# Attention into a top-1 expert layer, fp32, one core: the third batch's turn moved behind the values' products, and three smaller edits

## The chip, the cores and the metric

One core of one Trainium2 chip. The metric is the device time of one execution in microseconds (us); before the change it is 499.81 us, the median of three runs (499.52 to 500.13). Lower is better. Engine names: PE is TensorE's matmul side and PEld its weight loads, DVE is VectorE, ACT is ScalarE, POOL is GpSimd, and SP is the queue of SyncE that issues most transfers.

## The reference

Four batches of 12 heads, 448 positions, 64 values per head: softmax attention whose scores pass through a tanh cap. Its output, 1792 tokens of 768 values, goes through a top-1 layer of eight experts.

```python
scores = (q @ k.transpose(0, 1, 3, 2)) / 8
scores = cap * np.tanh(scores / cap)
attn = softmax(scores)                      # exp over its sum + 1e-9
x = (attn @ v).transpose(0, 2, 1, 3).reshape(1792, 768)
logits = x @ w_gate                         # 8 experts
e = argmax(logits)
out = softmax(logits)[e] * sigmoid(x @ w_output_gate)[e] * (relu(x @ w1[e]) @ w2[e])
```

Each token is computed by its one expert alone, and the expert's weights (w1 768x1024, w2 1024x768 in fp32) are read for the experts that have tokens.

## The kernel before

**Units.** The attention runs over 24 units u, six per batch; a unit is a pair of heads. `qk(u, s)` makes the transposed scores of one slice of keys (slices 0, 1 and 2 hold 128 keys of each head, slice 3 the last 64 of both) and ScalarE's tanh writes them to `pt` (L441). `expo(u)` is one exponential over the whole unit (L444). `pv(u, c)` multiplies by the values (L452), one unit behind the scores: in the loop, unit u's scores come first, then `pv(u - 1)`. `presum(u)` adds up the exponentials (GpSimd up to unit 19, VectorE from 20), and `sums(u)` is a product with a one-hot that collects these sums (L484). `u_evac` moves the values' product from PSUM to `ut`.

**The order is written by hand.** Each engine runs its instructions in the order in which this file emits them. Each unit has places "f", "g", "h", "q" and "e" (`slot(u, y)`): "f" and "g" stand after the scores and before the exponential, "h" after the exponential and before `pv(u - 1)`, "q" after `pv(u - 1)`, "e" at the end of the unit. `end_of_batch(b)` says, in the table `at`, which step of a batch's end goes to which place; a key (x, y) is unit 6(b + 1) + 1 + x, so that (0, ...) is unit 19 and (1, ...) unit 20 for the third batch (b = 2).

**A batch's end** turns the softmax sums into reciprocals, finds each token's expert and writes the token rows:
- `sums_out`: ScalarE copies the sums to `ssb` (L517); `sums_tr`: four PE transposes into `trec` (L522); `recips`: a VectorE reciprocal (L527)
- `gate_mm`, `gate_out`: gate products of three units (`tg`, L536) and ScalarE's copy `gsb` (L295); `gate_tr`, `gate_mul`: PE transposes `pg` (L551), each times the reciprocals on VectorE (L557)
- `logits`, `choose`: VectorE finds the expert (one-hot `ohb`)
- `rank_mm`: two small products with `tri` and `onesb` (`trk`, L597, L598), which also calls `exps` (two small ScalarE exponentials); `place`, `place2`, `enter`: VectorE turns them into table places (`posi`) and entries (`ent`, L629); `scatter`: four indirect GpSimd writes to the tables (L637)
- `row_tr(p)`, `row_out(p)`: for each of six head pairs four PE transposes into `trow` (L646), a VectorE product with the reciprocals into `xr` (L651), and a store of `xr` to `xs` in DRAM, issued on SP when `store_rows` is called (L658). `xr` has three buffers. In the first two batches every other pair is turned on VectorE instead (`row_v`, L682, L684, store L690), with reciprocals from `recips_b` (L677)

**PSUM banks.** In the third batch these PE results take two banks in turn, B and C (`extra`): B is also the bank of slice 1 of the next unit's scores, C that of slice 3. A transposition or a score product into such a bank waits until VectorE or ScalarE has read what stood in it.

**The start.** `load_nat(0)` loads the first keys and queries on the SP and ACT queues; PE turns them (`nat_k`, L414; `nat_q`, L420), and `first_planes(0)` splits them into a high and a low part (K0H, K0L, QH, QL; L295 or L297 and L303). The 64 last keys of the unit are its tails.

**The expert layer.** 13 blocks of 128 tokens (`mm1`, `mm2`, L1175) run on PE; weights come through SP into `raw1`, `raw2` and are split by ScalarE (L1153) and VectorE (L1154) into `wr`. Six smaller rests run beside them (`mm_h`, L1315). Three of the six (`OWN`) have weights of their own, `rh`, six pieces of w1 and eight of w2, loaded on GpSimd's queue (L1291) by `pump`, which is called after each chunk of products and issues one piece at a time when its buffer is used up. `gather_h(k)` fetches a rest's tokens on the same queue (L991 to L1006).

Of the kernel before, what the change touches and what calls it, by code (L numbers as in the profile page):

```python
# [9 lines left out]
F32 = mybir.dt.float32  # L10
# [12 lines left out]
def tile_kernel(ctx: ExitStack, tc, q, k, v, cap, w_gate, w_ogate, w1, w2, out):  # L23
    nc = tc.nc
    B, H, S, D = q.shape
# [74 lines left out]
    NK = 3  # L100
# [10 lines left out]
    def load_natural(dst, src, n, m, engs, lo=0):  # L111
        for j in range(2):
            o = lo if j == 0 else 0
            engs[j].dma_start(out=dst[:, 0:n, j], in_=src[j, o:o + n * m].rearrange("(c p) d -> p c d", c=n))

    def load_nat(u, engs):
        (k0, q0), k_, q_ = nat[u], heads(k, u), heads(q, u)
        load_natural(k0, k_, NK, 128, engs, T0)
        r0, n = u * S, NP * S + SK
        engs[1].dma_start(out=k0[0:64, NK], in_=k.rearrange("b h s d -> (b h s) d")[r0:r0 + 2 * n]  # L120
                          .rearrange("(j r) d -> r j d", j=2)[0:T0])
        load_natural(q0, q_, NCH, CP, engs)

    KT, QT = (0, 1, 4), (2, 3, 5)
    kview = [raw1[i].rearrange("p (h r a) -> p h r a", h=2, a=32) for i in KT]
# [167 lines left out]
    def copy(act, dst, src):  # L293
        if act:
            nc.scalar.activation(out=dst, in_=src, func=ACTF.Copy)  # L295
        else:
            nc.vector.tensor_copy(out=dst, in_=src)  # L297
# [4 lines left out]
    def minus(out, x, y):  # L302
        nc.vector.tensor_tensor(out=out, in0=x, in1=y.bitcast(F32), op=ALU.subtract)  # L303
# [33 lines left out]
    def first_planes(u, mid=lambda: None):  # L337
        ts, (main, *tails) = k_parts(u, nat_k(u))
        if u:
            copy(False, main[0], main[2])  # L340
            minus(main[1], main[2], main[0])
        mid()
        q_, (q0,) = q_parts(u, nat_q(u))
        if u:
            copy(False, q0[0], q0[2])
        else:
            copy(True, main[0], main[2])
            copy(True, q0[0], q0[2])
            minus(main[1], main[2], main[0])
            scales()  # L350
        minus(q0[1], q0[2], q0[0])
        for x, z, y in tails:
            copy(False, x, y)
            minus(z, y, x)
        pl[u] = ts + q_

    def t_k(u):
        pl[u] = planes_of(k_parts(u, turned(ldk.pop(u), SK + 128)))
# [50 lines left out]

    def nat_k(u):  # L410
        pk = tbank([128, S], "tk0")
        for c in range(NK + 1):
            n = min(128, S - c * 128)
            nc.tensor.transpose(pk[:, c * 128:c * 128 + n], nat[u][0][0:n, c].rearrange("p j d -> p (j d)"), ident[0:n, 0:n])  # L414
        return pk
# [87 lines left out]
    def end_of_batch(b):  # L503
# [166 lines left out]
        def recips_b():  # L670
            ps = tbank([128, S], "tks")
            nc.vector.transpose(out=ps, in_=rt["ssb"])
            r = T("recb", [128, NP // 2, NB])
            t = ps.rearrange("p (t r) -> p r t", r=32)
            for a in range(4):
                g = 2 + a // 2
                nc.vector.reciprocal(out=r[32 * a:32 * a + 32], in_=t[32 * g:32 * g + 32, 0:NP // 2])  # L677

        def row_v(p):
            nrow[0] += 1  # L680
# [21 lines left out]
        if b < B - 2:  # L702
            at = {(-2, "q"): [g0], (0, "q"): [g1], (0, "e"): [sums_out], (1, "g"): [t[1], rws[0]], (1, "e"): [recips_b],
                  (2, "e"): [rws[1]], (3, "g"): gts, (3, "e"): [rws[3]], (4, "g"): [rws[2]], (4, "h"): [logits, choose],
                  (5, "g"): [rank_mm, place, place2, rws[4]], (5, "h"): [enter], (6, "e"): [rws[5]]}
            for i, x in enumerate(((6, "g"), (8, "g"), (9, "g"), (10, "g")) if b == 0 else ((6, "g"),) * NCH):
                at.setdefault(x, []).append(P(scatter, (i,)))
        elif b == B - 2:
            g = early()
            nx = P(next, g, None)  # L710
            lds = [P(load_raw, 0, w, c) for w in range(2) for c in range((KD, KF)[w])]
            fd = [P(fetch_dma, i) for i in range(NE)]
            at = {(-2, "q"): [g0], (0, "f"): [P(sums, EARLY), g1, sums_out], (0, "h"): [t[1], *gts, logits, choose],
                  (1, "g"): [rws[0], rank_mm, place], (1, "h"): [place2, enter, scatter], (1, "q"): [rws[1], rws[2], rws[3], store_rows],
                  (2, "g"): [rws[4], rws[5]], (2, "h"): [store_rows, P(v_main, NU - 2, nc.sync), P(v_tails, NU - 2, nc.sync), *[nx] * 6, P(set_known, NE)],
                  (2, "q"): [fd[0], P(v_main, NU - 1, nc.sync), *lds[:2], fd[1]],
                  (3, "h"): [P(gather, 0), P(gather, 1), *lds[2:KD]],
                  (3, "e"): [fd[2], *lds[KD:KD + 2], fd[3]], (4, "f"): lds[KD + 2:]}
# [340 lines left out]
    for u in range(NU):  # L1059
# [7 lines left out]
        if u > 0:  # L1067
            load_ahead()
        if u == 0:
            first_planes(1, lambda: qk(0, NK))  # L1070
        else:
            qk(u, NK if u < NN else 2)
# [220 lines left out]

    def pump():

        if rsp and len(hraw) < len(hseq):
            w = hseq[len(hraw)][0]
            if sum(x[0] == w for x in hraw) - hused[w] < (KD, KF)[w]:
                load_h(len(hraw) + 1)
# [151 lines left out]
```

## Time and profile before

| | |
|---|---|
| median of three runs | 499.81 us |
| the profiled execution | 501.27 us, of which 499.7 us from the first to the last instruction |
| mean granted TensorE clock in it | 0.996 |
| busy, share of the span | PE 97%, DVE 76%, ACT 74%, POOL 59% |

The attention takes the first 189 us of the span, the expert layer the rest. A line of a timeline reads: start in us, duration in us, engine, line of the kernel, operation, tile written <- tiles read, shapes, how many instructions are merged (x4), and in brackets how long the engine sat idle before it and what released it. A product of fp32 tiles counts twice (two passes), so that three products are x6.

### The profile page before, as it was taken

To read this page: it belongs to the slowest core of one execution; us is meant where nothing else is said; L and a number is where in the kernel's file an instruction comes from. 1 tells how busy PE (TensorE), PEld (TensorE's weight loads), DVE (VectorE), ACT (ScalarE), POOL (GpSimd) and SP (SyncE) were. 2 spreads that over 40 slices of the span, in tenths; PEclk is the share of its full clock that TensorE was granted. 3 is DMA by queue.
4 is the path that set the end of the run, shared out by engine and by line. 5 is a ranking of instruction groups with operands and counts; after the bars stand their busy time and mean duration, and the time that the engine had idled before them with its cause. 6 is when DMAs were issued, how large, how long until landed. Compare 5 with 4: busy or idle time off the path is not lost. (4 is left out here: it accounts for less than half of the span.)

```text
span 499.7 us, 9942 instructions
## 1 busy us (share of the span) xinstructions
PE 484.3 (97%) x3040; PEld 335.9 (67%) x3040; DVE 380.4 (76%) x688; ACT 370.0 (74%) x433; POOL 296.0 (59%) x310
## 2 busy tenths in 40 slices
PE   7999999999989999999999999999999899999994
PEld 6544445445445535789998888978799667686691
DVE  6788899999978888999988969758595656565440
ACT  5999999899897797375798878857586666584551
POOL 7899999898998345573758643138356053522001
PEclk9999999999999999999999999999999999999998
DMA  7776777677573669870795263194889599791001
GB/s 175 117 140 114 125 126 136 113 133 115 106 127 55 118 184 335 275 254 1 253 391 220 95 221 134 57 361 168 281 268 407 202 355 411 272 383 46 0 34 53
DMA packets 158590, 91.95 MB, mean 184 GB/s; under 512 B 141234, under 2 KB 141370, under 8 KB 158528
## 3 DMA queue, kind: packets, MB, share of 16 engines
q1 hardware_dynamic: 148544, 58.24, 44.6%
q0 software_dynamic: 8832, 32.74, 17.7%
q8 instruction: 26, 0.43, 0.4%
q10 hardware_dynamic: 1152, 0.25, 0.2%
q14 instruction: 36, 0.29, 0.2%
HBM read 123.68 MB, written 12.04 MB: 272 GB/s over the span
## 5 line engine op out<-in xcount | busy, mean ns | idle before, releaser
L1154 DVE TENSOR_TENSOR wr<-raw,wr 128x768 fp32r<-128x768 f32 (+1 forms) x167 | 171.6, 1066 | 66.4 <-ACT wr L1153 65.6
L1153 ACT ACTIVATE wr<-raw 128x768 fp32r<-128x768 f32 (+1 forms) x167 | 150.3, 935 | 27.4 <-PE py L1175 11.0
L441 ACT ACTIVATE pt<-s,icap 128x896 f32<-128x896 f32 (+1 forms) x95 | 79.4, 917 | 9.2 <-PE s L434 8.2
L452 PE MATMUL u<-pt,vv 128*64 128x448 f32 x384 | 78.2, 546 | 0.5 <-ACT pt L444 0.3
L1175 PE MATMUL py<-wr,hh 128*128 128x384 f32 x352 | 77.3, 340 | 0.0
L1175 PE MATMUL php<-wr,xh 128*128 128x512 f32 x264 | 74.8, 405 | 0.0
L1244 POOL DMA_INDIRECT out_dram<-yo,ti x13 | 20.9, 1610 | 86.3 <-ACT yo L1242 72.3
L444 ACT ACTIVATE pt<-pt,capc 128x3136 f32<-128x3136 f32 x24 | 69.9, 2913 | 0.6
L1175 PEld LDWEIGHTS py<-wr,hh 128*128 128x128 f32 x352 | 61.2, 188 | 4.0 <-issue 3.7
L1175 PEld LDWEIGHTS php<-wr,xh 128*128 128x128 f32 x264 | 47.4, 188 | 12.8 <-issue 2.8
L452 PEld LDWEIGHTS u<-pt,vv 128*64 128x64 f32 x384 | 25.6, 136 | 40.5 <-issue 35.9
L465 POOL TENSOR_TENSOR pb<-pb,pt 64x448 f32<-64x448 f32 x40 | 45.7, 1143 | 3.1
L460 POOL TENSOR_TENSOR pb<-pt 128x896 f32<-128x896 f32 x20 | 42.3, 2113 | 7.8 <-ACT pt L444 4.1
L1175 PE MATMUL py<-wr,hl 128*128 128x384 f32 x176 | 44.8, 335 | 0.0
L461 POOL TENSOR_TENSOR pb<-pb,pt 128x896 f32<-128x896 f32 x20 | 42.1, 2105 | 1.6
L1175 PE MATMUL php<-wr,xl 128*128 128x512 f32 x132 | 41.5, 395 | 0.0
L1291 POOL DMA_DIRECT2D rh<-in_moe_w_dram x42 | 23.2, 555 | 17.3 <-DVE wr L1154 7.8
L1175 PEld LDWEIGHTS py<-wr,hl 128*128 128x128 f32 x176 | 31.8, 188 | 0.0
L1175 PEld LDWEIGHTS php<-wr,xl 128*128 128x128 f32 x132 | 24.8, 188 | 6.0
L1345 POOL DMA_INDIRECT out_dram<-yh,toh x6 | 7.8, 1300 | 34.9 <-ACT wr L1153 16.7
L953 POOL DMA_INDIRECT xg<-xs,ti x14 | 19.8, 1416 | 6.7 <-POOL ti L946 3.8
L637 POOL DMA_INDIRECT tab<-ent,posi x16 | 16.4, 1024 | 9.2 <-DVE ent L629 4.8
(334 smaller groups left out, 825.1 us busy)
## 6 DMA issues: line engine op xcount, KB each, us to landing
raw<-in_moe_w_dram SPq DMA_DIRECT2D x78, 512.0 KB
raw<-in_moe_w_dram SPq DMA_DIRECT2D x104, 384.0 KB
rh<-in_moe_w_dram POOLq DMA_DIRECT2D x18, 512.0 KB, 8.0
rh<-in_moe_w_dram POOLq DMA_DIRECT2D x24, 384.0 KB, 10.2
raw<-in_q_dram SPq DMA_DIRECT2D x45, 112.0 KB
raw<-in_k_dram SPq DMA_DIRECT2D x84, 56.0 KB
vv<-in_v_dram SPq DMA_DIRECT2D x48, 96.0 KB
xs<-xr SPq DMA_DIRECT2D x24, 112.0 KB
```

Of the source, the lines that this page charges most:

```text
L441: nc.scalar.activation(out=pt[u][:, 2 * s:2 * s + n], in_=ps, func=ACTF.Tanh, scale=icap)
L444: nc.scalar.activation(out=pt[u], in_=pt[u], func=ACTF.Exp, scale=capc)
L452: nc.tensor.matmul(ups[u][64 * j:64 * j + 64], lhsT=V[:, c, j, :], rhs=P[:, 2 * c + (j if c < NK else 0)], start=(c == 0), stop=(c == NK))
L460: eng.tensor_tensor(out=s1[u], in0=P[:, 0:2], in1=P[:, 2:4], op=ALU.add)
L461: eng.tensor_tensor(out=s1[u], in0=s1[u], in1=P[:, 4:6], op=ALU.add)
L465: eng.tensor_tensor(out=s1[u][h, j], in0=s1[u][h, j], in1=P[h, 2 * NK], op=ALU.add)
L953: nc.gpsimd.indirect_dma_start(out=g, out_offset=None, in_=xs[0:n], in_offset=bass.IndirectOffsetOnAxis(ap=ti, axis=0), bounds_check=n - 1 ...
L1153: nc.scalar.activation(out=t[:, 0, 0:F], in_=raw, func=ACTF.Copy)
L1154: nc.vector.tensor_tensor(out=t[:, 1, 0:F], in0=raw, in1=t[:, 0, 0:F].bitcast(F32), op=ALU.subtract)
L1175: nc.tensor.matmul(ps[g][:, 0:n], lhsT=st[:, c], rhs=w[:, z, g * n:(g + 1) * n], start=(c == 0 and st is hi and z == 0), stop=(c == (KD, K ...
L1244: nc.gpsimd.indirect_dma_start(out=out, out_offset=bass.IndirectOffsetOnAxis(ap=ti, axis=0), in_=y, in_offset=None, bounds_check=NT - 1, o ...
L1291: nc.gpsimd.dma_start(out=d, in_=rows_of(src, e, w, c), **kw)
```

## The change

1. **Third batch (b = 2).** `gate_mm(1)` now comes before `sums_out` and `gate_out(1)` after it, so ScalarE copies `ssb` first. The transposes of the sums, the reciprocals, the gates' turns, `logits` and `choose` move from (0, "h") to (0, "q"): behind `pv(18)`. `rank_mm`, `place`, `place2`, `enter` and `scatter` move from (1, "g") and (1, "h") to (1, "q"): behind `pv(19)`.
2. **First queries ahead.** Of unit 0 the queries are loaded before the keys' tails. The tails are turned and split by themselves (`tail0`), after the first three slices' scores; VectorE, no longer ScalarE, makes the first keys' high part; the scales follow the queries' split.
3. **Fewer reciprocals.** `recips_b` (first two batches) takes one reciprocal of 64 partitions and four copies in place of four reciprocals of 32.
4. **Rests' weights two by two.** `pump` may issue two pieces in one call, once a rest of `OWN` has begun.

```diff
         r0, n = u * S, NP * S + SK
+        if u == 0:
+            load_natural(q0, q_, NCH, CP, engs)
         engs[1].dma_start(out=k0[0:64, NK], in_=k.rearrange("b h s d -> (b h s) d")[r0:r0 + 2 * n]
                           .rearrange("(j r) d -> r j d", j=2)[0:T0])
-        load_natural(q0, q_, NCH, CP, engs)
+        if u:
+            load_natural(q0, q_, NCH, CP, engs)
...
         else:
-            copy(True, main[0], main[2])
+            copy(False, main[0], main[2])
             copy(True, q0[0], q0[2])
             minus(main[1], main[2], main[0])
+        minus(q0[1], q0[2], q0[0])
+        if not u:
             scales()
-        minus(q0[1], q0[2], q0[0])
-        for x, z, y in tails:
+        for x, z, y in tails if u else ():
             copy(False, x, y)
             minus(z, y, x)
         pl[u] = ts + q_
+
+    def tail0():
+        pk = ps_m.tile([128, S], F32, tag="sm", name="tk0t")
+        nc.tensor.transpose(pk[:, SK:S], nat[0][0][0:64, NK].rearrange("p j d -> p (j d)"), ident[0:64, 0:64])
+        hi, lo = kpl[0]
+        for j in range(2):
+            h, c = slice(64 * j, 64 * j + 64), slice(SK + 64 * j, SK + 64 * j + 64)
+            copy(False, hi[h, c], pk[h, SK:S])
+            minus(lo[h, c], pk[h, SK:S], hi[h, c])
...
-        for c in range(NK + 1):
+        for c in range(NK + (u > 0)):
...
+            x = T("recx", [64, NP // 2, NB])
+            nc.vector.reciprocal(out=x, in_=t[64:128, 0:NP // 2])
             for a in range(4):
-                g = 2 + a // 2
-                nc.vector.reciprocal(out=r[32 * a:32 * a + 32], in_=t[32 * g:32 * g + 32, 0:NP // 2])
+                g = a // 2
+                nc.vector.tensor_copy(out=r[32 * a:32 * a + 32], in_=x[32 * g:32 * g + 32])
...
-            at = {(-2, "q"): [g0], (0, "f"): [P(sums, EARLY), g1, sums_out], (0, "h"): [t[1], *gts, logits, choose],
-                  (1, "g"): [rws[0], rank_mm, place], (1, "h"): [place2, enter, scatter], (1, "q"): [rws[1], rws[2], rws[3], store_rows],
+            at = {(-2, "q"): [g0], (0, "f"): [P(sums, EARLY), P(gate_mm, 1), sums_out, P(gate_out, 1)],
+                  (0, "q"): [t[1], *gts, logits, choose],
+                  (1, "g"): [rws[0]], (1, "q"): [rank_mm, place, place2, enter, scatter, rws[1], rws[2], rws[3], store_rows],
...
         if u == 0:
+            tail0()
             first_planes(1, lambda: qk(0, NK))
...
-        if rsp and len(hraw) < len(hseq):
+        for _ in range(2 if hused[0] else len(rsp[:1])):
+            if len(hraw) == len(hseq):
+                return
             w = hseq[len(hraw)][0]
             if sum(x[0] == w for x in hraw) - hused[w] < (KD, KF)[w]:
                 load_h(len(hraw) + 1)
```

**What moves on TensorE, units 19 and 20.** `sm` are the sums, `tg` the gate products, `u` the values' product, `s` scores. Before:

```order
L484 MATMUL sm<-pb,ohc 32x448 x4
L536 MATMUL tg<-ut,wg 32x448 x3
L522 MATMUL trec<-ident,ssb 112x128 x4
L551 MATMUL pg<-ident,gsb_1859 112x96
...
L452 MATMUL u<-pt,vv_121 64x448 x8
L434 MATMUL s<-QH,K0H 128x448 x2
...
L646 MATMUL trow<-ident,ut 112x128 x4
L597 LDWEIGHTS tri
...
L452 MATMUL u<-pt,vv_121 64x448 x8
L646 MATMUL trow<-ident,ut 112x128 x12
L434 MATMUL s<-QH,K1H 128x448 x2
```

Changed:

```order
L497 MATMUL sm<-pb,ohc 32x448 x4
L549 MATMUL tg<-ut,wg 32x448 x3
L465 MATMUL u<-pt,vv_121 64x448 x8
L535 MATMUL trec<-ident,ssb 112x128 x4
L564 MATMUL pg<-ident,gsb_1864 112x96
...
L447 MATMUL s<-QH,K0H 128x448 x2
...
L659 MATMUL trow<-ident,ut 112x128 x4
L465 MATMUL u<-pt,vv_121 64x448 x8
L610 LDWEIGHTS tri
...
L659 MATMUL trow<-ident,ut 112x128 x12
L447 MATMUL s<-QH,K1H 128x448 x2
```

The values' product comes ahead of `trec` and of the gates' turns in unit 19, and ahead of the rank's two products in unit 20. VectorE's order of work in these two units is the same as before.

**What moves on VectorE at the start.** `tk` are the turned keys, `tq` the turned queries, `tk0t` the turned tails. Before:

```order
L303 TENSOR_TENSOR K0L<-tk_269,K0H 128x384
L187 RECIPROCAL icap<-capc 128x1
L188 TENSOR_SCALAR icap<-icap 128x1
L303 TENSOR_TENSOR QL<-tq_274,QH 128x448
L297 CAST K0H<-tk_269 64x64
...
L297 CAST K1H<-tk_345 128x384
```

Changed:

```order
L300 CAST K0H<-tk_269 128x384
L306 TENSOR_TENSOR K0L<-tk_269,K0H 128x384
L306 TENSOR_TENSOR QL<-tq_273,QH 128x448
L190 RECIPROCAL icap<-capc 128x1
...
L300 CAST K0H<-tk0t 64x64
...
L300 CAST K1H<-tk_346 128x384
```

The first keys' cast is new on VectorE, the queries' split is next but one, and the tails wait for a transpose of their own.

**What moves on GpSimd's queue**, at the second and the third rest of `OWN`. Before:

```order
L1291 DMA rh_5_3238<-in_moe_w_dram 128x768
L991 TENSOR_TENSOR tch<-tch 64x4
...
L1006 DMA xgh<-xs,toh 128x384
L1291 ISA
L1291 DMA rh_6_3239<-in_moe_w_dram 128x768
```

Changed:

```order
L1308 DMA rh_5_3243<-in_moe_w_dram 128x768
L1308 ISA
L1308 DMA rh_6_3244<-in_moe_w_dram 128x768
...
L1308 DMA rh_7_3245<-in_moe_w_dram 128x768
L1007 TENSOR_TENSOR tch<-tch 64x4
...
L1022 DMA xgh<-xs,toh 128x384
```

The last two pieces of a rest's w2 go ahead of the next rest's tokens (`xgh`). Nothing else changes its place on this queue.

## Rows read from the trace of the kernel before

**Rows 1.** Page, part 1: busy us, share of the span, instructions.

```profile
PE 484.3 (97%) x3040; PEld 335.9 (67%) x3040; DVE 380.4 (76%) x688; ACT 370.0 (74%) x433; POOL 296.0 (59%) x310
```

**Rows 2.** TensorE's timeline, units 19 to 21.

```profile
147.62 0.93 PE L536 MATMUL tg<-ut,wg 128*32 128x448 f32 x6
149.72 0.65 PE L522 MATMUL trec<-ident,ssb 128*112 128x128 f32 x4 [1.17 <-ACT ssb L517]
...
150.96 3.23 PE L452 MATMUL u<-pt,vv 128*64 128x448 f32 x16
154.12 0.47 PE L434 MATMUL s<-QH,K0H 64*128 64x448 f32 x2
...
160.94 1.09 PE L646 MATMUL trow<-ident,ut 128*112 128x128 f32 x8
162.38 0.65 PE L646 MATMUL trow<-ident,ut 128*112 128x128 f32 x4 [0.35 <-DVE xr L651]
...
164.18 0.47 PE L434 MATMUL s<-QH,K1H 64*128 64x448 f32 x2 [0.35 <-DVE xr L651]
```

**Rows 3.** ScalarE's timeline, unit 19.

```profile
148.60 0.54 ACT L295 ACTIVATE gsb<-tg 96x448 f32<-96x448 f32 x1 [0.47 <-PE tg L536]
149.04 0.62 ACT L517 ACTIVATE ssb<-sm,epsc 128x448 f32<-128x448 f32 x1
```

**Rows 4.** VectorE's timeline, units 19 to 21.

```profile
150.40 0.46 DVE L527 RECIPROCAL rec<-trec 112x48 f32<-112x48 f32 x1 [1.98 <-PE trec L522]
...
158.33 0.68 DVE L651 TENSOR_TENSOR xr<-trow,rec 112x512 f32<-112x512 f32 x1
...
160.83 0.18 DVE L629 RECIPROCAL ent<-den 112x4 f32<-112x4 f32 x1
161.63 1.29 DVE L651 TENSOR_TENSOR xr<-trow,rec 112x512 f32<-112x512 f32 x2 [0.62 <-PE trow L646]
163.43 0.69 DVE L651 TENSOR_TENSOR xr<-trow,rec 112x512 f32<-112x512 f32 x1 [0.52 <-DMA xs<-xr]
...
169.18 0.69 DVE L651 TENSOR_TENSOR xr<-trow,rec 112x512 f32<-112x512 f32 x1 [0.91 <-DMA xs<-xr]
```

**Rows 5.** SP's queue: stores of token rows, issues merged.

```profile
158.45 1.93 SPq L690 DMA_DIRECT2D xs<-xr  x4
160.47 10.27 SPq L658 DMA_DIRECT2D xs<-xr  x12
```

**Rows 6.** All engines' timeline, the first 12 us.

```profile
5.11 0.17 DVE L207 MEMSET raw<- 64x128 f32 x1
...
5.72 0.58 PE L420 MATMUL tq<-ident,raw 112*128 112x112 f32 x4 [0.60 <-DMA raw<-in_q_dram]
...
6.92 0.62 DVE L303 TENSOR_TENSOR QL<-tq,QH 128x448 fp32r<-128x448 f32 x1 [0.41 <-ACT QH L295]
...
7.46 0.21 DVE L297 CAST K0H<-tk 64x64 fp32r<-64x64 f32 x1
...
8.11 3.35 ACT L441 ACTIVATE pt<-s,icap 128x896 f32<-128x896 f32 x4 [1.22 <-PE s L434]
...
9.90 0.47 PE L439 MATMUL s<-QH,K0H 128*128 128x448 f32 x1
...
10.01 0.56 DVE L297 CAST K1H<-tk 128x384 fp32r<-128x384 f32 x1 [1.22 <-PE tk L414]
...
11.48 2.91 ACT L444 ACTIVATE pt<-pt,capc 128x3136 f32<-128x3136 f32 x1
```

**Rows 7.** Line L677: durations in ns (least, median, most), first and last start, shapes.

```profile
L677 DVE RECIPROCAL recb<-tks x8: 416/422/427, 69.6 to 114.6; 32x42 f32<-32x42 f32 x8
```

**Rows 8.** Line L1315, the rests' products: one of the waits before them.

```profile
  DMA rh<-in_moe_w_dram: 0.7, 2
```

**Rows 9.** TensorE's timeline around 400 us.

```profile
400.01 0.44 PE L965 MATMUL pt_x<-ident,xg 128*128 128x128 f32 x2 [1.34 <-ACT xth L1020]
```

## The prediction

> **What bounds the kernel.** I read the page first: TensorE is busy 97% of the span [rows 1], so a change can only pay, or cost, where TensorE waits. Next I took TensorE's timeline for its idle times. Four bear on this change: 0.60 us for the first queries, 1.17 us ahead of the third batch's `trec`, twice 0.35 us in the rows of unit 20 and before unit 21's scores, and 1.34 us in the expert layer [rows 2, 6, 9]. Then I followed each to the engine that ended it. The 1.17 us end with ScalarE, which copies `gsb` first (and waits 0.47 us for the gate products) and `ssb` after it [rows 3]. The two waits of 0.35 us end with VectorE's row products [rows 2], and one of these waits in turn for the store of an earlier row [rows 4, 5]. So at units 19 to 21 three things take turns: TensorE, VectorE's long chain, and the stores of rows.
>
> **Part 1, the third batch: TensorE's gain.** Before, the gate products end at 147.62 + 0.93 = 148.55, TensorE idles to 149.72, `trec` and the gates' turns take 150.96 - 149.72 = 1.24, and `pv(18)` takes 154.12 - 150.96 = 3.16 until unit 20's scores [rows 2]. Now `pv(18)` follows the gate products at about 148.5: its exponentials and values are older than that. `trec` starts at 148.5 + 3.16 = 151.66 and unit 20's scores at 151.66 + 1.24 = 152.90, a lead of 154.12 - 152.90 = 1.22 us. ScalarE's swap saves the 0.47 us of waiting for the gates [rows 3]; it is off the path now, since `ssb` is ready long before 151.66.
>
> **Part 1: what VectorE loses.** Its reciprocal waits for `trec`. It started at 150.40, that is 0.68 after `trec` [rows 2, 4]; now it starts at 151.66 + 0.68 = 152.34, which is 1.94 us later, and VectorE has idled that much longer. Its order of work is unchanged, so everything behind the reciprocal moves by 1.94: the gates, the expert's choice, a turn for unit 23, the last row of the second batch, row 0 of the third (158.33), the places and `ent` (160.83) [rows 4]. From the reciprocal to `ent` it has no wait that could swallow this.
>
> **Part 1: where the two meet.** TensorE reaches the rows of unit 20 at 160.94 - 1.22, about 159.7 [rows 2]. There row 1's turn goes into bank B, which holds row 0's turn until VectorE has read it: 158.33 + 0.68 + 1.94 = 160.95. Row 2's waits for the places, row 3's for row 1's product. The 0.62 us that VectorE waited for row 1's turn [rows 4] go, so rows 1 and 2 come only some 1.3 later than before. Row 3's product decides. Its buffer is row 0's, whose store has to land, and SP issues that store behind the four pieces of the second batch's last row: 158.45, 160.47, landing by 163.43 [rows 4, 5]. All of this hangs on VectorE's chain, so 163.43 becomes 163.43 + 1.94 = 165.37. Unit 21's second slice of scores needs the bank that this product frees: 164.18 becomes 166.1. From here to the expert layer TensorE's timeline shows no longer wait than these 0.35, and ScalarE's and GpSimd's steps follow it. **So the lead of 1.22 turns into a loss of 1.94.** The least that this part can cost, if the store does not bind: row 3's product then follows its turn, which follows row 1's product (161.63 + 0.69, 1.3 later, so 163.6; a turn and its latency as from `trec` to the reciprocal, 0.68), at 164.3, or 0.9 late. The whole gain, had VectorE no say, would be the 1.22 and both waits of 0.35: 1.9. I take +1.94, since each step of the store's chain has its row.
>
> Here a rule stands against the change. First the row: row 5's product waited 0.91 us for a store to land, although row 2's store, which it needs, was issued by about 164.5 (rows 1 and 2 are done at 162.3 and 162.92, and four issues of some 0.5 us follow) [rows 4, 5]; it landed some 5 us after its issue, row 0's some 2.5 after. The Trainium skill, "SBUF — State Buffer", section "SBUF: two separate sides", says that GpSimd cannot write the descriptors of its transfers while VectorE holds the port pair which the two share, and that the transfer engines then sit idle. By it, VectorE's sums for unit 20 beside the four table writes held this store; in the changed kernel these sums come later and the writes do not, so the wait of 0.91 may go. This would bring the early plan of the expert layer forward, and TensorE's sum stays as it is, since row 3 decides it. By the row alone the wait stays.
>
> **Part 2, the start.** The queries' wait of 0.60 goes, since their second half is issued one place earlier. But VectorE now makes K0H itself: it is free at 5.11 + 0.17 = 5.28 [rows 6], a cast of this shape takes 0.56 (0.59 with the step to the next), K0L as long, so QL starts at about 6.5 in place of 6.92 [rows 6]. The first tanh can start 0.42 earlier, at 7.69. It then runs 3.35 over four slices, of which the last starts some 2.7 in, at 10.4. This last slice needs the tails, which before were split long ahead (7.46 on) and now wait for their own transpose behind the third slice's scores: transpose at about 8.8, four small VectorE steps of 0.25 from 9.1, the third done at 9.8, the fourth at 10.06, three products to 10.7 (9.90 to 10.8 before). The last tanh starts at 10.75, takes 0.64, and the exponential starts at 11.4, against 11.48 [rows 6]. **Gain 0.06**; between 0.42, if the tails come in time, and a loss of 0.2, if the transpose is late. Next in line is the second unit's cast at 10.01, about 0.1 later; ScalarE, busy with the exponential until 14.4, covers it.
>
> **Part 3, fewer reciprocals.** Eight of 0.42 us [rows 7] become two and eight copies. No copy of this shape is in the trace: at most the 0.42 of the reciprocal it replaces (then the part costs 0.42 a batch), at least nothing (then 1.3 a batch are saved). I take a saving of 0.8 a batch on VectorE. TensorE does not wait for VectorE in these units (its four waits stand above), and the splits made here are for units several places ahead: **0**. If that cover were gone, 1.6 would be won.
>
> **Part 4, the rests' weights.** The pieces that go first are the sixth and seventh of a rest's w2, ahead of one gather of tokens. TensorE waited for these weights 0.7 us in all, twice [rows 8]: **0.1** gained, at most 0.7. The gather behind them comes later by two pieces and is not needed until the rest's turn, chunks later. The 1.34 us at 400 [rows 9] end with ScalarE, held by experts' weights on the other queue; its load is the same.
>
> **Sum.** +1.94 - 0.06 - 0.1 = +1.8. The profiled execution took 501.27 us, so the changed one would take 503.1 so profiled. It lies 1.46 above the median of the three runs, 499.81; the same shift gives **501.6 us**.
>
> **Rivals.**
> - *TensorE keeps its lead.* Price: 1.2 to 1.9 gained, 497.9 to 498.6. For it: TensorE's longest wait in the attention goes, and it is the engine at 97%. It decides by row 3's product: if that ends by 163 or so, unit 21's scores start ahead of 164.18. Against it: VectorE would have to shed 1.9 us and has only its two waits, 0.62 and 0.52. Chance 0.2.
> - *A smaller loss.* Either the store does not bind (+0.9, so 500.5), or the loss is partly taken back downstream, as where TensorE waits 1.34 at 400 (down to +0.5, so 500.3): it would be, if the weights it waits for came on time of their own. Against: their buffers are freed by TensorE's own progress. Chance 0.25.
> - *The stores stick.* Row 0's store now goes out around 162.4 to 163, close to the first table write. If it lands only with the others, at 169.2, row 3's product is 3.8 later still: 505.4. By the skill's rule above this needs VectorE's sums beside the writes, and they now start behind that very product, so I give it little. Chance 0.05.
>
> **How the numbers follow.** The loss as summed has 0.5; its own range, from a store that lands a little earlier to a turn that is a little later, is 500.8 to 502.4. A measurement of this kernel can tell 0.2%, that is 1 us, from no change: faster is below 498.8, slower above 500.8. Faster has 0.2 (the first rival), the same 0.25 (the second), slower 0.55. The range goes from 498.4 (into the first rival) to 502.8; left out are the rest of that rival and the sticking stores.
>
> **What would show it.** Right: TensorE goes from the gate products straight into `pv(18)`; VectorE's third-batch reciprocal starts near 152.3 after almost 4 us of idle time; unit 20's scores start near 152.9; before rows 1 and 3 and before unit 21's second slice TensorE idles about 1 us each, released by VectorE's `xr`; the exponential of unit 21 starts about 1.9 later than before, that of unit 0 at its old time. Wrong: if that exponential starts earlier than before, VectorE's chain is shorter than I read it; if the first exponential starts by 11.1, the tails were no hindrance.

## The result: slower by 5.8 us, three times what was forecast

| | before | changed |
|---|---|---|
| median of six runs each, us | 499.97 (499.50 to 500.47) | 505.25 (504.76 to 507.35) |
| ratio, 95% interval | | 1.0116 (1.0102 to 1.0129) |
| the profiled execution, us (span) | 501.27 (499.7) | 504.92 (503.3) |

1.16% of 500 us are 5.8 us (5.1 to 6.4); the two medians differ by 5.3, as the ratio is not their quotient. Forecast were 1.8, and the range ended 2.5 us below the median. The page of the changed kernel, its part 1, beside [rows 1]:

```profile
PE 486.1 (97%) x3040; PEld 336.5 (67%) x3040; DVE 384.8 (76%) x691; ACT 370.5 (74%) x432; POOL 295.8 (59%) x310
```

VectorE is busy 4.4 us longer with three instructions more, although eight reciprocals of 0.42 us became two and eight copies. TensorE, with the same instructions, is 1.8 us longer in them.

To see where the time went I compared the starts of the 24 exponentials (one a unit, on ScalarE). Changed less before: -0.23 us from the first to that of unit 10, +2.2 at unit 11, +3.3 from unit 12 to 17, +2.7 at 18, +1.7 at 20, +4.7 from 21 on. So there are **two losses**: one at units 11 and 12, where the prediction had none, and one at unit 21, where it had its whole loss.

**The first loss** begins on VectorE, where part 3 puts its copies. VectorE's timeline of the changed kernel around 70 us, and GpSimd's beside it:

```profile
69.38 0.42 DVE L689 RECIPROCAL recx<-tks 64x42 f32<-64x42 f32 x1
69.84 1.60 DVE L692 COPY recb<-recx 32x42 f32<-32x42 f32 x1
...
71.46 2.37 DVE L692 COPY recb<-recx 32x42 f32<-32x42 f32 x3
...
73.86 0.59 DVE L313 STREAM_TRANSPOSE tk<-raw 128x384 f32<-128x384 f32 x1
```

```profile
69.25 2.15 POOL L473 TENSOR_TENSOR pb<-pt 128x896 f32<-128x896 f32 x1
71.48 2.11 POOL L474 TENSOR_TENSOR pb<-pb,pt 128x896 f32<-128x896 f32 x1
73.67 2.40 POOL L478 TENSOR_TENSOR pb<-pb,pt 64x448 f32<-64x448 f32 x2
```

The first copy begins during GpSimd's addition of 69.25 and ends at 71.44, when that addition does (71.40). The next, of 0.18, begins at 71.46, between two additions; the third lasts from 71.65 to 73.64, when the next addition (71.48 and 2.11) has ended, and the fourth follows in 0.18. The line's durations (ns: least, median, most) say the same of all eight:

```profile
L692 DVE COPY recb<-recx x8: 175/178/2199, 69.8 to 116.9; 32x42 f32<-32x42 f32 x8
```

A copy alone takes 0.18 us; one that begins during an addition lasts until the addition is over. In the first batch four copies take 3.99 us, where the four reciprocals took 1.73 (4 x 0.43, [rows 7]). VectorE has no idle time in the 10 us after that, so its gate products of this batch come late. Before they started at 81.50. Changed:

```profile
84.01 1.01 DVE L570 TENSOR_TENSOR gm<-pg,rec 112x384 f32<-112x384 f32 x2
```

TensorE's timeline with unit 11's scores, before:

```profile
82.94 0.37 PE L434 MATMUL s<-QH,K1H 64*128 64x448 f32 x2
...
84.46 0.47 PE L434 MATMUL s<-QH,K1H 64*128 64x448 f32 x2
...
89.00 0.96 PE L484 MATMUL sm<-pb,ohc 128*32 128x448 f32 x8
```

and of the changed kernel:

```profile
82.50 0.36 PE L447 MATMUL s<-QL,K1H 64*128 64x448 f32 x2
84.61 0.48 PE L447 MATMUL s<-QH,K1H 64*128 64x448 f32 x2 [1.75 <-DVE gm L570]
...
86.23 0.73 PE L447 MATMUL s<-QH,K1H 64*128 64x448 f32 x2
...
88.66 3.72 PE L465 MATMUL u<-pt,vv 128*64 128x448 f32 x16
92.31 0.96 PE L497 MATMUL sm<-pb,ohc 128*32 128x448 f32 x8
```

The second slice needs the bank that the gate products read; TensorE idles 1.75 us. That isn't all: at 86.23 a pair of products takes 0.73 where the pair at 84.61 took 0.48. The windows of 2 us (length, per engine busy us and count, then the granted clock, DMA share, GB/s):

```profile
84.00:86.00 2.00, 1.39 (x9) 0.97 (x9) 1.97 (x5) 0.47 (x1) 1.92 (x2) 1.00 0.70 114
86.00:88.00 2.00, 2.00 (x10) 1.19 (x9) 1.86 (x5) 1.33 (x3) 1.92 (x2) 0.57 1.01 161
88.00:90.00 2.00, 2.00 (x10) 0.89 (x10) 1.93 (x3) 1.97 (x2) 1.68 (x2) 0.58 0.97 148
```

After the idle time the granted clock falls to 0.57, near the lower of its two levels (1.2 of 2.4 GHz), for some 3.4 us. From 86.23 to the sums at 92.31 TensorE needs 6.08 us, before (84.46 to 89.00) 4.54 for the same work: 1.54 more. The idle time puts this slice 1.90 us later than before (84.61 for 82.94, with the 0.23 of the start); with the 1.54 that is all but 0.1 of the 3.5 us (from -0.23 to +3.3). This is how the profiled execution lost them. Three of the six ran at a mean granted clock of 0.994 to 0.998 and took 504.76 to 505.77 us all the same; what they lost instead of the clock is in no trace.

**The second loss** is the one that was worked out. TensorE's timeline, units 19 to 21, beside [rows 2]:

```profile
150.30 0.93 PE L549 MATMUL tg<-ut,wg 128*32 128x448 f32 x6
151.15 3.23 PE L465 MATMUL u<-pt,vv 128*64 128x448 f32 x16
154.31 0.65 PE L535 MATMUL trec<-ident,ssb 128*112 128x128 f32 x4
...
155.55 0.47 PE L447 MATMUL s<-QH,K0H 64*128 64x448 f32 x2
...
163.72 0.65 PE L659 MATMUL trow<-ident,ut 128*112 128x128 f32 x4 [0.66 <-DVE xr L664]
...
166.33 0.65 PE L659 MATMUL trow<-ident,ut 128*112 128x128 f32 x4 [1.14 <-DVE xr L664]
...
168.86 0.47 PE L447 MATMUL s<-QH,K1H 64*128 64x448 f32 x2 [1.07 <-issue]
```

From the gate products to unit 20's scores it takes 5.25 us, 6.50 before: a lead of 1.25 (forecast 1.22). Then TensorE idles 0.66, 1.14 and 1.07 us where [rows 2] have twice 0.35. VectorE's timeline, beside [rows 4]:

```profile
155.00 0.46 DVE L540 RECIPROCAL rec<-trec 112x48 f32<-112x48 f32 x1 [3.83 <-PE trec L535]
...
165.59 0.69 DVE L664 TENSOR_TENSOR xr<-trow,rec 112x512 f32<-112x512 f32 x1
166.56 0.69 DVE L664 TENSOR_TENSOR xr<-trow,rec 112x512 f32<-112x512 f32 x1 [0.28 <-DMA xs<-xr]
168.11 0.69 DVE L664 TENSOR_TENSOR xr<-trow,rec 112x512 f32<-112x512 f32 x1 [0.85 <-DMA xs<-xr]
```

The reciprocal starts 4.70 after the gate products, 2.78 before: 1.92 later (forecast 1.94). Row 3's product still waits for row 0's store.

### The profile page after: what moved, and what is told of

It reads as the page before. It is cut to its first block, busy times and chain, and to the rows that moved or that the text cites. A ratio compares the mean times of both kernels' runs of the same rounds, so it can differ in the third digit from the quotient of the medians.

```text
span 503.3 us, 9947 instructions
## 1 busy us (share of the span) xinstructions
PE 486.1 (97%) x3040; PEld 336.5 (67%) x3040; DVE 384.8 (76%) x691; ACT 370.5 (74%) x432; POOL 295.8 (59%) x310
## 5 line engine op out<-in xcount | busy, mean ns | idle before, releaser
L465 PE MATMUL u<-pt,vv 128*64 128x448 f32 x384 | 77.9, 548 | 0.5 <-ACT pt L457 0.3
L465 PEld LDWEIGHTS u<-pt,vv 128*64 128x64 f32 x384 | 25.6, 138 | 41.3 <-issue 36.0
L1364 POOL DMA_INDIRECT out_dram<-yh,toh x6 | 6.2, 1038 | 38.1 <-DMA raw<-in_moe_w_dram 16.1
L650 POOL DMA_INDIRECT tab<-ent,posi x16 | 17.5, 1091 | 9.2 <-DVE ent L642 4.8
```

Of the source, the lines that this page charges most:

```text
L465: nc.tensor.matmul(ups[u][64 * j:64 * j + 64], lhsT=V[:, c, j, :], rhs=P[:, 2 * c + (j if c < NK else 0)], start=(c == 0), stop=(c == NK))
```

## Experiments

Twelve kernels, each timed in five rounds (5 to 12 executions) beside the kernel before on the same chip. Ratios are to that kernel (median 499.44 us beside the first move alone, the second move alone, the swap with four row buffers and all that should pay; 499.15 beside the other eight). The last column is from each profile: the start of the last exponential less that of the first, compared with the run of parts 2 and 4 alone (170.52 us). This leaves out the start of the kernel and the expert layer.

| kernel | median us | ratio (95%) | attention, us |
|---|---|---|---|
| before | 499.97 | 1 | +0.6, a wait of 0.70 that is told of below |
| changed | 505.25 | 1.0116 (1.0102 to 1.0129) | +5.5, low clock at 86 |
| without part 3 | 501.43 | 1.0045 (1.0026 to 1.0064) | +1.9 |
| part 3 alone | 503.49 | 1.0085 (1.0067 to 1.0102) | +2.9 |
| reductions for copies | 502.04 | 1.0051 (1.0033 to 1.0069) | +3.7, low clock at 162 |
| part 1 alone | 502.69 | 1.0063 (1.0041 to 1.0085) | +3.4, low clock at 165 |
| first move alone | 502.37 | 1.0046 (1.0025 to 1.0068) | +2.7 |
| second move alone | 500.25 | 1.0007 (0.9984 to 1.0031) | +1.4, low clock at 162 |
| four row buffers | 501.01 | 1.0039 (1.0022 to 1.0057) | +2.0, low clock at 163 |
| parts 2 and 4 | 499.34 | 1.0006 (0.9994 to 1.0017) | 0 |
| swap alone | 499.21 | 1.0002 (0.9989 to 1.0016) | -0.4 |
| swap, parts 2 and 4 | 498.65 | 0.9994 (0.9983 to 1.0004) | -0.2 |
| swap, four row buffers | 499.72 | 1.0000 (0.9978 to 1.0022) | -1.3 |
| all that should pay | 500.03 | 1.0008 (0.9986 to 1.0030) | -1.1 |

### Part 3: is it the copies?

**Without part 3.**

```diff
-            x = T("recx", [64, NP // 2, NB])
-            nc.vector.reciprocal(out=x, in_=t[64:128, 0:NP // 2])
             for a in range(4):
-                g = a // 2
-                nc.vector.tensor_copy(out=r[32 * a:32 * a + 32], in_=x[32 * g:32 * g + 32])
+                g = 2 + a // 2
+                nc.vector.reciprocal(out=r[32 * a:32 * a + 32], in_=t[32 * g:32 * g + 32, 0:NP // 2])
```

> The change without its third part (the four reciprocals of 32 partitions are back in the first two batches). Theory A, copies held by GpSimd: in the trace of the changed kernel a copy of recb takes 0.18 us alone and 1.6, 2.0 and 2.2 us while GpSimd adds up exponentials, the first batch's gate products on VectorE come 2.5 us later for it, and TensorE idles 1.75 us at 84.61 and then runs at a lower granted clock. Without part 3 that wait goes: the exponential of unit 12 starts at about 94.8 (98.3 with the change, 95.03 before), and some 3 us come back: 502 us, 1.003 to 1.005 of the kernel before, the rest being part 1. Theory B, the wait at 84.61 has another cause (the transfers or the shifted start of part 2): 505 us, the wait stays.

Measured: 501.43 us, ratio 1.0045. The wait at 84.61 is gone, and the exponential of unit 12 starts at 94.83. Theory A holds, B falls; 5.8 - 2.25 = 3.5 us of the loss were part 3's (2.4 to 4.7 by the two intervals).

**Part 3 alone**, the same lines put into the kernel before.

> The kernel before with part 3 alone. Theory A (copies held by GpSimd, VectorE 2.3 us later in the first batch, TensorE idle 1.8 us and then 1.5 us lost at the lower clock, 0.7 us of it swallowed at 133 where the kernel before waits for values): 2.5 to 3.5 us slower than before, 1.005 to 1.007. Theory B (the copies are harmless by themselves): within 0.2% of before. What the prediction on record said of this part: no change.

Measured: ratio 1.0085, 3.3 to 5.1 us slower, most of it above theory A's 2.5 to 3.5. The profiled execution was the fastest of the five (501.94; the others 503.35 to 503.95), so what the others lost beyond it isn't shown. In its profile the copies take 4.06 us in the first batch and TensorE idles 1.78 us for the gates, with the granted clock at 1.00:

```profile
84.91 0.47 PE L434 MATMUL s<-QH,K1H 64*128 64x448 f32 x2 [1.78 <-DVE gm L557]
```

In the second batch, which cost the changed kernel nothing, the copies take 3.63 and TensorE idles another 0.57 at 131.06. How long a copy is held depends on where in GpSimd's addition it falls.

**The copies as reductions.**

```diff
-                nc.vector.tensor_copy(out=r[32 * a:32 * a + 32], in_=x[32 * g:32 * g + 32])
+                nc.vector.tensor_reduce(out=r[32 * a:32 * a + 32], in_=x[32 * g:32 * g + 32].unsqueeze(3), axis=AX.X, op=ALU.add)
```

> The change, with the four copies of part 3 written as reductions over an axis of one element: same source, same target, same number of elements, another operation of VectorE. Theory A (what is slow is the copy's way of reading and writing beside GpSimd): each takes about 0.2 us whatever GpSimd does, no wait at 84.61, and the time is that of the change without part 3, about 502 us or a little less. Rival A2 (any small instruction that reads the reciprocals just written in SBUF, or that changes partitions, is held there): 1 to 2 us each as with the copies, and 505 us.

Measured: 502.04 us, as the change without part 3 (501.43) within the intervals. Its VectorE and GpSimd at the same place, and the line's durations:

```profile
70.02 0.79 DVE L692 TENSOR_REDUCE recb<-recx 32x42 f32<-32x42 f32 x4
```

```profile
69.51 2.17 POOL L473 TENSOR_TENSOR pb<-pt 128x896 f32<-128x896 f32 x1
```

```profile
L692 DVE TENSOR_REDUCE recb<-recx x8: 184/188/191, 70.0 to 113.9; 32x42 f32<-32x42 f32 x8
```

All four run beside the same addition, 0.19 us each. Source, target and size are the copies'; only the operation differs. So neither the reciprocal just written nor the change of partitions is slow (rival A2 falls): it is the copy, as an operation beside GpSimd. The Trainium skill, "SBUF — State Buffer", section "SBUF: two separate sides", says that VectorE and GpSimd share a pair of ports under an exclusive lock, that whichever starts first keeps it for its whole instruction, and that an fp32 copy from SBUF to SBUF takes both pairs; "Who interferes with whom" on that page says that reductions never do on this chip. The trace agrees on both: up to 2.20 us against 0.18, and 0.19 throughout.

### Part 1: where is the lead lost?

**Part 1 alone**: its table entries in the kernel before.

> The kernel before with part 1 alone (third batch behind the values' products). Theory C, that of the prediction: the lead of 1.2 us at unit 20 turns into a loss of 1.9 us at unit 21 by VectorE's chain and the store of row 0: exponential of unit 21 at 169.7 (167.76 before), and 0.5 to 1.9 us slower at the end (part of it may be taken back in the expert layer, where the trace of the changed kernel has lost a wait of 1.3 us). Rival D (all of the loss was part 3, part 1 pays): exponential of unit 21 at 166.5 or earlier, 1.2 us faster.

Measured: ratio 1.0063, 2.0 to 4.2 us slower; unit 21's exponential at 170.53, later than either theory said. Rival D falls. The surplus over theory C shows in the windows of TensorE at 164 us (length, busy, count, granted clock, DMA share, GB/s), first this kernel:

```profile
164.00:166.00 2.00, 0.91 (x8) 0.92 0.94 185
166.00:168.00 2.00, 2.00 (x9) 0.50 0.88 152
168.00:170.00 2.00, 2.00 (x13) 0.73 0.05 2
```

and the change without part 3, all engines:

```profile
164.00:166.00 2.00, 0.92 (x10) 0.48 (x6) 1.46 (x2) 1.01 (x1) 1.39 (x3) 1.00 0.92 181
166.00:168.00 2.00, 2.00 (x14) 1.26 (x13) 1.93 (x3) 1.70 (x3) 1.70 (x2) 1.00 0.84 140
```

Both idled alike: 0.63, 0.20, 1.14 and 1.09 us within 6 us. TensorE's timeline of the change without part 3:

```profile
162.76 0.65 PE L659 MATMUL trow<-ident,ut 128*112 128x128 f32 x4 [1.14 <-DVE xr L664]
...
165.29 0.47 PE L447 MATMUL s<-QH,K1H 64*128 64x448 f32 x2 [1.08 <-DVE xr L664]
...
167.71 1.08 PE L659 MATMUL trow<-ident,ut 128*112 128x128 f32 x8
```

In part 1 alone the granted clock then fell to 0.50, in this one it stayed. From unit 21's second slice to the turns of the rows 4 and 5 part 1 alone needs 3.91 us (165.47 to 169.38), the change without part 3 2.42 (165.29 to 167.71): the fall costs 1.5 us. It comes in some executions and not in others, as their mean granted clocks say. The six kernels with one or both of part 1's moves and without the copies ran 55 times; in 29 of these the mean granted clock was 0.993 or less, and they took 1.2 to 2.3 us longer in the mean than the other runs of the same kernel. Of 58 runs of the five kernels with neither moves nor copies, 2 were so, and none of the 82 runs of the kernel before beside them. Where the clock fell is shown for the four of the six that have a fall in their profile (between 162 and 166 us); for the other executions it is inferred from the mean.

**The first move alone** (turns of the sums, gates and choice behind unit 19's product; the rank in its old place).

```diff
-                  (1, "g"): [rws[0]], (1, "q"): [rank_mm, place, place2, enter, scatter, rws[1], rws[2], rws[3], store_rows],
+                  (1, "g"): [rws[0], rank_mm, place], (1, "h"): [place2, enter, scatter], (1, "q"): [rws[1], rws[2], rws[3], store_rows],
```

> The change without part 3, and with the rank, the places and the scatter back in front of the values' product of unit 20: of part 1's two moves the first alone (turns of the sums, gates, choice behind the product of unit 19). Theory C: the reciprocal of the third batch still comes at 151.5 (150.40 before, 148.79 with the swap alone), everything behind it on VectorE as late, and the loss is that of the change without part 3: 501 us, exponential of unit 21 near 168.9. Rival G: the loss came from the second move (rank's products late, VectorE waiting for them): then this is at 499.3 or below.

Measured: ratio 1.0046, that of the change without part 3 (1.0045); reciprocal at 152.13, unit 21's exponential at 169.57, 0.7 later than expected, as this execution also waited for values at unit 17, which the next section tells of. Theory C holds, G falls.

**The second move alone** (the rank behind unit 20's product).

```diff
-                  (0, "q"): [t[1], *gts, logits, choose],
+                  (0, "h"): [t[1], *gts, logits, choose],
```

> The other half: turns of the sums and choice in front of the product of unit 19 again (reciprocal near 148.9), rank, places and scatter behind that of unit 20. Theory C: rank's two products then end about 159.3, VectorE, done with row 0 at about 157.5, waits some 2 us for them, and the rows 1 to 3 come as late as in the change without part 3, less some tenths: 0.5 to 1.5 us slower than the swap alone (499.21). Rival G (this is where all of part 1's loss comes from): 501 us or more.

Measured: ratio 1.0007, somewhere between 0.8 us faster and 1.5 slower: the time alone doesn't settle its size, but G falls. The trace has the wait: VectorE, done with row 0, idles for the rank's products.

```profile
159.50 0.76 DVE L626 TENSOR_TENSOR pre<-pre,trk 128x8 f32<-128x8 f32 x4 [1.53 <-PE trk L611]
```

So this move costs VectorE 1.53 us when its chain is early; after the first move the chain is too late for it to matter.

**Four row buffers** in the change without part 3 (`nrow[0] % 4` for `nrow[0] % 3`, twice).

> The change without part 3 (501.4 us, ratio 1.0045) with four buffers of token rows in place of three, so that row 3 of the third batch no longer waits for the store of row 0. The prediction on record said that this store decides the loss (without it 0.9 us would be lost in place of 1.94). If so, VectorE's wait of 0.84 before row 3's product goes, the exponential of unit 21 comes some 0.8 us earlier than the 168.87 of that run, and the time falls by 0.8, more if TensorE's granted clock then stays up. Rival F (the turns of the rows on TensorE, each waiting for the product of the row before it, take their place): less than 0.3 us.

Measured: 501.01 us, 0.4 below the run without part 3, within the intervals. VectorE's wait for row 0's store is gone, but the turn of row 3, which waits for row 1's product, has taken part of its place: 0.60 us, of which 0.45 are the turn's own slowness (1.10 for 0.65). TensorE and VectorE of this kernel:

```profile
163.08 1.10 PE L659 MATMUL trow<-ident,ut 128*112 128x128 f32 x4 [1.14 <-DVE xr L664]
```

```profile
164.21 0.69 DVE L664 TENSOR_TENSOR xr<-trow,rec 112x512 f32<-112x512 f32 x1 [0.60 <-PE trow L659]
```

Here too the clock fell, from the idle 1.14 us on. From this turn to the next rows' (168.10) it is 5.02 us; without part 3 4.95, of which 1.08 are idle, so the clock costs 5.02 - 3.87 = 1.15, an estimate that takes it that nothing would have waited here at the full clock. The attention's +2.0 less that is +0.9, which is what the prediction gave as the price "if the store does not bind". By this estimate the store decides between 0.9 and 1.94, as forecast; that the time itself falls by 0.8 is not shown.

### What of the change pays?

**Parts 2 and 4.**

> The change without parts 1 and 3: the start and the rests' weights alone. By the prediction 0.16 us faster (0.06 and 0.1), at most 1.1; by the trace of the changed kernel the start gives 0.23. So 498.9 to 499.1 beside a median of 499.15, no change that can be told; a slower one by over 0.5 us would mean that part 4 costs something in the expert layer, which no trace so far shows.

Measured: ratio 1.0006 (0.9994 to 1.0017): no change, as expected. The first exponential starts at 11.54 here, 11.25 in the changed kernel; over the nine profiles with part 2 it lies between 11.23 and 11.65, over the five without between 11.44 and 11.74, so the gain of 0.23 that I had read from one profile is mostly scatter between executions.

**The swap alone**: ScalarE copies `ssb` first, all else as before.

```diff
-            at = {(-2, "q"): [g0], (0, "f"): [P(sums, EARLY), g1, sums_out], (0, "h"): [t[1], *gts, logits, choose],
+            at = {(-2, "q"): [g0], (0, "f"): [P(sums, EARLY), P(gate_mm, 1), sums_out, P(gate_out, 1)], (0, "h"): [t[1], *gts, logits, choose],
```

> The kernel before with one piece of part 1: ScalarE copies ssb ahead of gsb; the turns of the sums, the gates and the rank stay in front of the values' products. Theory C (in part 1 the swap is the gain and the move behind the products is the loss, by way of VectorE's reciprocal): in the run of part 1 alone ssb was ready at 147.9, ahead of the end of the gate products at about 148.5, so trec starts there without the wait of 1.17, the reciprocal of the third batch comes about 1 us earlier than before (149.3 to 149.6, before 150.40), and with it the rows: exponential of unit 21 about 1 us earlier than before (166.7, before 167.76). Time 0.5 to 1.2 us faster than before. Rival E (VectorE or the store of row 0 holds the rows of unit 20 anyway): the lead of 1.2 us shows at unit 20 and is gone at unit 21: no change.

Measured: ratio 1.0002 (0.9989 to 1.0016), no change that can be told. VectorE's timeline:

```profile
148.79 0.46 DVE L527 RECIPROCAL rec<-trec 112x48 f32<-112x48 f32 x1 [1.53 <-PE trec L522]
...
161.85 1.29 DVE L651 TENSOR_TENSOR xr<-trow,rec 112x512 f32<-112x512 f32 x2 [1.15 <-DMA xs<-xr]
```

The reciprocal comes 1.6 us earlier than in [rows 4] (0.6 of it by a wait that only that execution has, see below), and TensorE's wait of 1.17 is gone, but the products of the rows 2 and 3 now wait 1.15 us for an earlier row to be stored, in place of 0.52. Rival E is nearer: 0.4 us are left at the end of the attention, and none in the time.

**The swap with parts 2 and 4.**

> Parts 2 and 4 with the swap, without the rest of part 1 and without part 3: what is left if only the paying pieces are kept. By theory C the sum of the two runs beside it, 0.7 to 1.5 us faster than before (about 498 us). By rival E no change.

Measured: 498.65 us, ratio 0.9994 (0.9983 to 1.0004): the lowest median of all, and no difference that can be told.

**The swap with four row buffers.**

> The kernel before with ScalarE's swap and four buffers of token rows. In the run of the swap alone TensorE led by 1.0 us at unit 20 and lost 0.6 of it at unit 21, where VectorE waited 1.15 us for the store of row 0 before row 3's product. If that wait is what takes the gain away, it goes here: exponential of unit 21 at 166.0 to 166.3 (166.77 with the swap alone), and the time is 0.5 to 1 us below that run's 499.21. If the turns of the rows take its place (each waits for the product before it), 0.2 us or less.

Measured: the exponential of unit 21 at 166.15, as expected (the profiled execution took 500.94 us, 1.2 above the median): the store's wait is down to 0.32 and the attention is 1.3 us shorter. The time is not (1.0000, 0.9978 to 1.0022). TensorE's timeline at the start of the expert layer:

```profile
191.68 0.73 PE L1175 MATMUL php<-wr,xl 128*128 128x512 f32 x2 [1.41 <-DVE xl L967]
...
196.48 0.77 PE L965 MATMUL pt_x<-ident,xg 128*128 128x128 f32 x5 [0.70 <-DMA xg<-xs,ti]
```

GpSimd's timeline of this kernel, and then of the swap alone:

```profile
186.81 0.61 POOL L943 TENSOR_TENSOR tc<-tc 128x4 f32<-128x4 f32 x1 [4.35 <-DMA tc<-tab]
...
190.26 1.75 POOL L953 DMA_INDIRECT xg<-xs,ti  x1 [0.27 <-POOL xg L952]
```

```profile
184.63 0.20 POOL L943 TENSOR_TENSOR tc<-tc 128x4 f32<-128x4 f32 x1 [2.15 <-DMA tc<-tab]
...
187.50 1.12 POOL L953 DMA_INDIRECT xg<-xs,ti  x1 [0.27 <-POOL xg L952]
```

The second block's gather waits for the table to be read back and goes out 2.8 us later than with the swap alone, although its attention ended earlier. Two things in the traces bear on it, and no run settles it. With the swap and the fourth buffer VectorE begins its additions for unit 20 at 162.43, before GpSimd has ended its own (in the twelve traces without both they overlap by 0.06 us at most). GpSimd's last two additions (L465, from 160.97) take 3.55 us together, 2.34 with the swap alone: here the second takes 2.34 by itself, in place of 1.13, and VectorE's second addition 1.93 in place of 1.09 (163.54 here, 164.17 there). GpSimd's writes to the tables follow the pair, so they start at 164.80 in place of 163.39. But the profile of parts 2 and 4 has no such meeting, and there too the second gather goes out late, at 190.53, with TensorE waiting 0.61 us.

**All that should pay** (swap, four row buffers, parts 2 and 4, reductions for copies).

> Swap, four row buffers, parts 2 and 4, and part 3 with one-element reductions for copies: everything of the change in the form in which it should pay. By the theories so far 498 to 498.7 us, that is 0.5 to 1 us faster than before; part 3 in this form frees 0.55 us of VectorE a batch, which no wait of TensorE asks for, so nothing more than the run beside it. If it is slower than that run by over 0.5 us, one of the small parts costs something.

Measured: 500.03 us, ratio 1.0008 (0.9986 to 1.0030), no difference that can be told, and the median above the expected 498 to 498.7, with the same two waits (1.43 and 0.79) and the same meeting of additions in its profile. No version found here beats the kernel before.

## Why the prediction was wrong

**Part 3, the step that failed.** "No copy of this shape is in the trace: at most the 0.42 of the reciprocal it replaces": the copies took up to 2.20 us. The bound was an operation that does not meet GpSimd; the trace shows that it doesn't, since reciprocals ran at 0.42 while GpSimd was adding (before: four from 69.59 to 71.32, beside an addition from 69.04 to 71.15). The text cited the very section of the Trainium skill that tells of the shared ports ("SBUF — State Buffer", "SBUF: two separate sides"), and used it for stores alone. By the same rule a copy could have been estimated from rows: up to a whole addition of 2.1 us, for perhaps two of the four. The next sentence failed too: "TensorE does not wait for VectorE in these units: 0" was read from waits that were not there. What was wanted was how much later VectorE could come. Against before (with the start's -0.23 taken off) its gate products came 2.74 us later (84.01 for 81.50) and TensorE's second slice 1.90 (84.61 for 82.94): the slack was 0.84. The sign of "if that cover were gone, 1.6 would be won" was wrong with it. Part 3 cost some 3.5 us of the 5.8, where 0 stood.

**Part 1, the mechanism right and a term missing.** The lead of 1.22 measured 1.25; the reciprocal's delay of 1.94 measured 1.92; the loss of 1.94 at the end of the attention is 1.9 in the run without part 3 (beside parts 2 and 4; beside the profile before, with its waits of 0.6, it is 1.3), and the signs named in advance are there: 3.4, 3.8 and 4.5 us of idle time before the reciprocal (without part 3, changed, part 1 alone), about 1 us of TensorE's before rows 1 and 3 and the second slice. What was missing is that TensorE's idle time has a second price: after its waits of 0.63, 0.20, 1.14 and 1.09 us TensorE may run on at the lower clock, 1.5 us dearer; of the 16 executions of part 1 alone and of the change without part 3, 8 had a mean clock of 0.993 or less. So the change without part 3 costs 2.25 us (1.3 to 3.2), more than its 1.9: its seven executions at a higher mean clock took 501.06 us in the mean, 1.9 above the 499.15 of the kernel before, the three others 503.17. In the changed kernel's profile such a fall came after part 3's wait, and none after part 1's.

**Parts 2 and 4** were taken at -0.06 and -0.1, and together lie between 0.3 us faster and 0.85 slower. The tails were the hindrance that the text named: the last slice waits 0.21 us for them, though the first tanh starts at 7.55, not 8.11.

**The base.** The profiled execution before was not a usual one. Its wait of 0.91 before row 5 [rows 4] is in none of the other thirteen traces (at most 0.12 there), and its 1.34 at 400 us [rows 9] has no equal at that place in any; waits of its kind, 0.76 to 1.22 us, stand near 389 us in three of the others. A third wait I had not seen, as it stands in the weight loads within a product:

```profile
133.27 0.32 PEld L452 LDWEIGHTS u<-pt,vv 128*64 128x64 f32 x2 [0.43 <-DMA vv<-in_v_dram]
134.10 0.19 PEld L452 LDWEIGHTS u<-pt,vv 128*64 128x64 f32 x2 [0.52 <-DMA vv<-in_v_dram]
```

It lengthens that product by 0.70 and recurs in one other profile (the first move alone). This is the +3.3 to +2.7 at unit 18 in the list above: the changed kernel had no such wait. So the wait of 0.91, on which a rule was tried, tells nothing of the rule. Nor did the rule fit the case: as the prediction quotes it, it is about transfers that GpSimd issues, and row 2's store goes out on SP [rows 5].

## What to carry to other kernels

An instruction's price goes by whom it shares with, not by its elements alone: before a small VectorE copy between SBUF tiles is put beside long GpSimd work, look at the GpSimd row that runs there and price the copy at what is left of it, or write it as an operation that isn't held there (here a reduction). That TensorE does not wait for an engine now says nothing of how late that engine may come: measure the slack from the last instruction that TensorE needs to the point where it needs it. And a wait of TensorE can cost more than its length, since what follows may run at half the clock.

## What was not expected of the hardware

A VectorE copy of 32 x 42 numbers from SBUF to SBUF takes 0.18 us, or 1.2 to 2.2 us when one of GpSimd's additions (2.1 us) is under way, while a reduction of the same numbers takes 0.19 in both cases. Additions of both engines that meet are longer too: GpSimd's 2.34 us for 1.13, VectorE's 1.93 for 1.09 (the swap with four row buffers). After idle times of 0.63, 0.20, 1.14 and 1.09 us within 6 us, the granted TensorE clock fell to 0.50 in the profile of part 1 alone and stayed at 1.00 in that of the change without part 3; after a single wait of 1.75 it fell to 0.57 in the changed kernel, and after one of 1.78 it stayed at 1.00 in that of part 3 alone.
